# Sorted attention pairs: denominators stored as a 65th column of the row table, division after the read-back, numerators turned by VectorE, and plan points moved

## The chip, the cores and the metric

The kernel runs on one core of a Trainium2 chip. Five engines with in-order queues work side by side on that core: TensorE (PE in the profile, with its weight loads as PEld), VectorE (DVE), ScalarE (ACT), GpSimd (POOL) and SyncE (SP), which mostly issues DMAs. The metric is the device time of one execution in microseconds, lower being better. The kernel before takes 925.34 us as the median of three runs (924.95 to 927.41).

## The reference

The first stage is clustered attention, the second a hard-swish feed-forward network (FFN):

```
q, k, v: (4, 8, 768, 64) float32     centroids: (8, 16, 64)
q_assign = argmax_c(normalise(q) . normalise(centroids))      # per head, 16 clusters
k_assign = argmax_c(normalise(k) . normalise(centroids))
scores   = q k^T / 8, and -1e9 where q_assign != k_assign
attn     = softmax(scores);  attn_out = attn v
x   = attn_out as (4*768, 512)
h   = x w_in;  out = (h * clip(h + 3, 0, 6) / 6) w_out        # 512 -> 2048 -> 512
```

A query therefore attends only to the keys of its own cluster. Numerators (exp(scores) v) and denominators (the sum of exp(scores)) are formed apart, and their quotient goes to the FFN.

## The kernel before

The 32 heads are taken two at a time: 16 *pairs*, numbered 0 to 15 (`g`). Four pairs make one batch, and a batch can enter the FFN when its four pairs are done.

**Pairs 0 to 6** are done with the full 768 x 768 score matrix and a mask, in a first loop. This takes the first quarter of the run, together with decoding of the weights. **Pairs 7 to 15** (`FIRST` = 7, `SECOND` = 8) are *sorted*: the rows of q, k and v are written to DRAM tables in the order of their clusters, so that only a band around the diagonal has to be computed. A sorted pair passes these steps:

- `load_natural`, `turn_natural`, `cluster_scores`, `own_clusters`, `run_up`, `step_up`, `order`, `positions`: every token's cluster, and from it its row in sorted order (`pos`). `load_queries` and `load_keys` fetch the rows that are to be scattered.
- `scatter`: 24 indirect DMAs issued by POOL write the rows of q (`qd`) and of k and v (`kvd`) to DRAM in sorted order. Behind each stand three small memsets (`pause`). The first sorted pair's scatter runs in the first loop.
- `load_ranked` reads the sorted rows back: q and k as 32 x 32 blocks (`piece`), v as rows (`vs`). `turn_ranked` turns the blocks by VectorE's 32 x 32 block transpose into `xs`, features on partitions.
- `band_scores`, `band_values`, `key_adds`, `band_sums`: the band's exponentials, the numerators `bn` (features on partitions, tokens along the row), and the denominators `dn` (a row per head and half).
- `band_divide` (L1318): three PE transposes of `dn` (L1322) and six of `bn` (L1326) bring tokens onto partitions, VectorE takes the reciprocal (L1330) and multiplies in two halves (L1333) into `xr`.
- `keep_ranked` (L1340): two DMAs on SP's queue write `xr` to the DRAM tables `xsd`, 768 rows of 64 floats for each head.
- `gather` (L1193): 12 indirect DMAs issued by POOL read the rows of `xsd` in the original order into `xn`, each with a pause behind it.
- `turn_back` (L1345): six PE transposes through the PSUM tile `ps`, a copy by ACT (L1039) into `xt`, and a DMA to `xd`, from which the FFN loads its blocks (`load_block`, L577). Where the pair closes a batch, the batch's FFN items are appended to `fill`.

The PSUM pool of `ps`, `psum_s`, has one buffer in this stage. `band_scores`, `band_divide` and `turn_back` all use it. The SBUF pool `rowp` holds `bn`, `xr`, `xn` and `xt` under one tag in three buffers.

**What sets the order.** The order is written out by hand. `steps_of(g)` gives each step an offset; `late_plan` adds the pair's base (`AHEAD` = 38 plus `SLOT` = 29 for each pair behind pair 8; 6 for pair 7; two less for the last pair) and yields a list of *points*. The loop at L1573 goes through the points, issues the steps of a point, and then one FFN item from `fill`, except at two points of each slot (`busy`). An FFN item is half of an `up` (uX or uY, L709, with sums on VectorE, L720) or half of a `down` part (X or Y, L748). A block of 256 tokens has 8 `up` and 7 `down` parts, so 30 items. While `gating` holds, a point's steps are put off to the next. Behind the last point (263), what is left of `fill` runs: a rest of batch 2, then all of batch 3. `down`'s last part stores an output half on ACT's queue when `st["last"]` is set, else on SP's. ACT's queue also issues the loads of the kept weight sums `tx` (L595).

In the first loop, two score tiles make one step `n`, and twelve tiles a pair. At step 6 of a pair the next loads are issued (`load`, L1544), and `load_sums` inverts the denominators of batch 0 and lets its first FFN block be loaded, by way of functions put off from step to step (L523).

Of the kernel before, what the change touches and what calls it, by code (L numbers as in the profile page):

```python
# [17 lines left out]
C = 16  # L18
# [107 lines left out]
def fast_path(ctx, tc, ok, q, k, v, centroids, moe_w_in, moe_w_out, out):  # L126
# [380 lines left out]
    def load_sums(b):  # L507
        size = 2 * NCH
        tok = plain[:, NKT * b * size : (NKT * b + unsorted(b)) * size]
        nc.sync.dma_start(tok, st["sums", b].rearrange("k t s -> (k t s)").rearrange("(p n) -> p n", p=P))  # L510

        def invert():
            nc.vector.reciprocal(out=tok, in_=tok)
            nc.sync.dma_start(st["rd", b].rearrange("k t s -> (k t s)").rearrange("(p n) -> p n", p=P), tok)
            return complete

        def complete():
            if unsorted(b) == NKT:
                waiting.extend((b, m) for m in range(NHC))
                load_block()  # L520

        if b == 0:
            later.append(lambda: later.append(lambda wait=invert(): later.append(wait)))  # L523
        else:
            st["invert"], st["complete"] = invert, complete

# [108 lines left out]
    def ffn_items(b):  # L635
# [121 lines left out]
        def down(m, part):  # L757
# [33 lines left out]
            def end():  # L791
# [150 lines left out]
    def open_late():  # L942
# [249 lines left out]

    def gather(g):  # L1193
        pos = st["pos", g]
        xn = st["xn", g] = st["rowp"].tile([P, NCH, 2, D], F32, name="xn", tag="row")
        for t in range(2):
            for j in range(NCH):
                nc.gpsimd.indirect_dma_start(  # L1198
                    out=xn[:, j, t], out_offset=None, in_=rows["xsd", g, t],
                    in_offset=bass.IndirectOffsetOnAxis(ap=pos[:, 0, j, t : t + 1], axis=0),  # L1200
                )
                pause()
# [112 lines left out]
        for i in range(NCH):  # L1315
            st.pop(("be", g, i))

    def band_divide(g):  # L1318
        dn, bn = st.pop(("dn", g)), st.pop(("bn", g))
        pt = scratch([P, NHC, P], "pdt")  # L1320
        for i in range(NHC):
            nc.tensor.transpose(out=pt[:, i], in_=dn[:, i * P : (i + 1) * P], identity=ident)  # L1322
        ps = st["psum_s"].tile([P, 2, 512], F32, name="ps")
        for i in range(NCH):
            at = i % NHC * P
            nc.tensor.transpose(  # L1326
                out=ps[:, i // NHC, at : at + P], in_=bn[:, i // NHC, at : at + P], identity=ident
            )
        inv = inverses[:, g - FIRST]
        nc.vector.reciprocal(out=inv, in_=pt[:, :, 0 : P : 2 * C])  # L1330
        xr = st["rowp"].tile([P, NCH, 2, D], F32, name="xr", tag="row")
        for hf in range(2):
            nc.vector.tensor_tensor(  # L1333
                out=xr[:, hf * NHC : (hf + 1) * NHC],
                in0=ps[:, hf, 0:HALF].rearrange("p (i t d) -> p i t d", i=NHC, t=2),
                in1=inv[:, :, hf : 4 : 2].unsqueeze(3).to_broadcast([P, NHC, 2, D]), op=ALU.mult,
            )
        st["xr", g] = xr

    def keep_ranked(g):  # L1340
        xr = st.pop(("xr", g))
        for t in range(2):
            nc.sync.dma_start(ranked("xsd", g, t), xr[:, :, t])

    def turn_back(g):  # L1345
        xn = st.pop(("xn", g))
        st.pop(("pos", g))
# [13 lines left out]
    def steps_of(g):  # L1361

        first, last = g == SECOND, g == NPAIR - 1
        if first:
            plan = [
                (-38, load_queries), (-38, load_keys, 0), (-38, load_keys, 1),
            ]
        elif g == FIRST:
            plan = [(-6, lambda g: st.pop("signed")())]
        else:  # L1370
            plan = [
                (-52, load_natural, 1), (-51, load_natural, 0), (-46, turn_natural, 1), (-45, turn_natural, 0),
                (-42, cluster_scores), (-40, own_clusters), (-39, load_queries), (-39, run_up), (-38, step_up),
                (-36, load_keys, 0), (-35, order), (-34, positions), (-33, load_keys, 1),
            ]
        s = -37 if first else -30
# [10 lines left out]
        if last:  # L1387
            plan += [
                (1, band_scores, (0, 5), 1), (2, band_scores, (2,), 3), (3, band_scores, (4,)),
                (3, band_values, 0), (3, key_adds, 0, 1, 2), (4, key_adds, 0, 3), (5, band_values, 1),  # L1390
                (5, key_adds, 1, 1, 2), (6, key_adds, 1, 3), (8, band_sums), (9, band_divide), (10, keep_ranked),
                (11, gather), (24, turn_back),
            ]
# [103 lines left out]
    with tc.manual_schedule():  # L1497
# [24 lines left out]
        for n in range(0, total + lag_d + 2, 2):  # L1522
# [19 lines left out]
                prep.pop(0)()  # L1542
            if r == 6:
                load(g + 2, "q", "k")  # L1544
                load(g + 1, "v")
            if len(prep) > 1:
                prep.pop(0)()
# [410 lines left out]
```

## Time and profile before

| | |
|---|---|
| time of the profiled execution | 924.17 us |
| its span | 922.4 us |
| median of three runs | 925.34 us |
| PE busy | 895.6 us (97%) |
| DVE busy | 586.4 us (64%) |
| POOL busy | 600.1 us (65%) |
| ACT busy | 305.0 us (33%) |

The span runs from the first to the last instruction of the program, and the execution's time has 1.8 us around it. A group's row gives an engine, an operation, the tiles written and read, the count, then the busy time in us, the mean of one in ns, and the idle time of the engine just before it with what ended that. A row of the timeline gives a start, a length, and in brackets the idle time before it. A row of the windows gives, for each engine, its busy time in that stretch.

### The profile page before, as it was taken

Reading aid. Unit: us, or ns where it says so; the run is one execution under the profiler, and the core shown is the slowest. Engines: PE = TensorE matmul, PEld = TensorE weight load, DVE = VectorE, ACT = ScalarE, POOL = GpSimd, SP = SyncE. Lnnn points to the kernel's source line nnn. Section 1 sums busy time; section 2 is a strip of 40 time slices with the busy share of each in tenths; the row PEclk is TensorE's granted clock in tenths of the full one; section 3 lists DMA queues with packets and bytes.
Section 4 is the critical chain, followed back from the end, with each engine's and each line's share of the span. In section 5 each row is a group of like instructions: output and inputs, shape, how many; then the busy total and the mean of one; then the engine's idle time right before and its main releaser. Section 6 shows DMA issues by size and latency. Waiting matters only on the chain.

```text
span 922.4 us, 17421 instructions
## 1 busy us (share of the span) xinstructions
PE 895.6 (97%) x6131; PEld 701.4 (76%) x6131; DVE 586.4 (64%) x1373; ACT 305.0 (33%) x627; POOL 600.1 (65%) x1438
## 2 busy tenths in 40 slices
PE   8999999999999999999999999999999988999997
PEld 5444444657798797887977978978888878999996
DVE  5874898799787394693774855856744716445361
ACT  6888786651220322212222230321412201112120
POOL 3878899996867858787888777787886051203030
PEclk9999999999999999999999999999999999999999
DMA  6656666536769577593792954937635413233220
GB/s 178 169 154 170 174 186 186 160 98 136 199 165 197 134 182 152 151 238 89 185 216 79 223 110 140 236 102 172 160 108 132 122 42 111 88 83 102 63 64 28
DMA packets 248377, 131.06 MB, mean 142 GB/s; under 512 B 206972, under 2 KB 225816, under 8 KB 248280
## 3 DMA queue, kind: packets, MB, share of 16 engines
q1 hardware_dynamic: 224168, 81.22, 36.9%
q10 hardware_dynamic: 13744, 34.44, 13.5%
q0 software_dynamic: 10368, 14.18, 5.1%
q8 instruction: 51, 0.84, 0.4%
q14 instruction: 46, 0.38, 0.1%
HBM read 99.82 MB, written 29.97 MB: 141 GB/s over the span
## 4 chain that ended last, share of the span: by engine, by line
PE 48%; DVE 9%; DMA 4%; POOL 2%; issue 1%; ACT 1%; ACTq 0%; SPq 0%; DVEq 0%; POOLq 0%
PE Y L748 14%; PE uY L709 9%; PE X L748 9%; PE uX L709 8%; PE pv L1285 3%; PE ps L1228 2%; DMA tx<-td 2%; DVE g_sb L720 1%; DVE sx L720 1%; DVE g_sb L699 1%; DVE g_sb L541 1%; POOL xn L1198 1%; PE pv L1228 1%; PE pd L1309 1%; PE ps L1038 1%
## 5 line engine op out<-in xcount | busy, mean ns | idle before, releaser
L1198 POOL DMA_INDIRECT xn<-xsd,pos x108 | 106.7, 988 | 58.9 <-DMA xsd<-xr 29.3
L538 ACT ACTIVATE sx<-g_sb,half_c 128x512 f32<-128x512 f32 x88 | 63.6, 722 | 198.5 <-DVE g_sb L720 198.3
L1147 POOL MEMSET unread<- 128x1 f32 x972 | 102.3, 105 | 37.6
L699 POOL TENSOR_TENSOR g_sb<-g_sb 128x256 f32<-128x256 f32 x52 | 39.6, 783 | 118.7 <-DVE g_sb L541 117.6
L457 POOL TENSOR_TENSOR acc<-acc,ex 128x768 f32<-128x768 f32 x56 | 104.5, 1867 | 16.7 <-ACT ex L446 14.1
L1155 POOL DMA_INDIRECT qd<-qn,pos x96 | 98.1, 1022 | 20.0 <-issue 14.4
L1155 POOL DMA_INDIRECT kvd<-kvn,pos x96 | 95.5, 995 | 21.8 <-issue 21.8
L748 PE MATMUL X<-w_out_sb,g_sb 128*128 128x256 f32 x384 | 93.3, 387 | 1.5 <-DVE g_sb L541 1.4
L709 PE MATMUL uX<-xb,w_in_sb 128*128 128x128 f32 x704 | 93.0, 275 | 0.0
L748 PE MATMUL Y<-T,g_sb 128*128 128x256 f32 x384 | 88.5, 381 | 0.0
L748 PE MATMUL Y<-w_out_sb,g_sb 128*128 128x256 f32 x384 | 88.5, 381 | 0.0
L709 PEld LDWEIGHTS uX<-xb,w_in_sb 128*128 128x128 f32 x704 | 85.7, 192 | 0.0
L748 PEld LDWEIGHTS X<-w_out_sb,g_sb 128*128 128x128 f32 x384 | 71.7, 193 | 16.3 <-DVE g_sb L541 3.9
L748 PEld LDWEIGHTS Y<-w_out_sb,g_sb 128*128 128x128 f32 x384 | 72.2, 190 | 12.6 <-issue 2.7
L748 PEld LDWEIGHTS Y<-T,g_sb 128*128 128x128 f32 x384 | 72.0, 190 | 12.5 <-issue 2.7
L755 DVE TENSOR_TENSOR y<-y,Y 128x256 f32<-128x256 f32 x47 | 19.7, 420 | 92.7 <-PE Y L748 91.9
L720 DVE TENSOR_TENSOR sx<-uX,sx 128x128 f32<-128x128 f32 x176 | 50.7, 288 | 38.3 <-ACT sx L727 34.1
L423 PE MATMUL ps<-xf 64*128 64x384 f32 x336 | 68.8, 487 | 0.6 <-ACT ex L446 0.6
L720 DVE TENSOR_TENSOR g_sb<-uY,sx 128x128 f32<-128x128 f32 (+1 forms) x176 | 65.5, 413 | 0.2 <-DVE sx L720 0.2
L446 ACT ACTIVATE ex<-ps 128x768 f32<-128x768 f32 x84 | 63.7, 803 | 3.1 <-PE ps L423 2.6
L541 DVE SCALAR_TENSOR_TENSOR g_sb<-sx,g_sb 128x512 f32<-128x512 f32 x88 | 63.3, 722 | 2.0 <-ACT sx L538 2.0
L467 PE MATMUL pv<-ex,vt 128*64 128x384 f32 x336 | 63.5, 499 | 0.0
(228 smaller groups left out, 1723.7 us busy)
## 6 DMA issues: line engine op xcount, KB each, us to landing
tx<-td ACTq DMA_DIRECT2D x86, 384.0 KB
raw<-in_moe_w_in_dram SPq DMA_DIRECT2D x16, 512.0 KB
raw<-in_moe_w_out_dram SPq DMA_DIRECT2D x16, 512.0 KB
xb<-xd SPq DMA_DIRECT2D x12, 512.0 KB
out_dram<-y SPq DMA_DIRECT2D x44, 128.0 KB
piece<-qd SPq DMA_DIRECT2D x36, 96.0 KB
piece<-kvd SPq DMA_DIRECT2D x36, 96.0 KB
vs<-kvd SPq DMA_DIRECT2D x18, 192.0 KB
```

Source lines behind the costliest of these rows:

```text
L423: nc.tensor.matmul(st["ps", n][:, t, 0:HALF], lhsT=x[r, NCH + j], rhs=x[r, hf * NHC : (hf + 1) * NHC], start=first, stop=last, skip_group_ ...
L446: nc.scalar.activation(out=ex, in_=sc, func=ACT.Exp, scale=SM_SCALE)
L457: nc.gpsimd.tensor_tensor(out=acc, in0=acc, in1=ex, op=ALU.add)
L467: nc.tensor.matmul(pv[t * D : (t + 1) * D], lhsT=vt[:, t, j], rhs=ex[:, t], start=(j == 0), stop=(j == NCH - 1),)
L538: nc.scalar.activation(out=r, in_=h, func=ACT.Relu, bias=half_c, scale=1.0 / 6.0)
L541: nc.vector.scalar_tensor_tensor(out=g, in0=r, scalar=1.0, in1=h, op0=ALU.min, op1=ALU.mult)
L709: nc.tensor.matmul(dst, lhsT=w[:, kt], rhs=x(kt), start=(kt == 0), stop=(kt == HK - 1))
L720: nc.vector.tensor_tensor(out=out_, in0=in0, in1=in1, op=ALU.add)
L748: nc.tensor.matmul(bank[:, half * HC : (half + 1) * HC], lhsT=g_sb[:, kind, i], rhs=w[:, i], start=(first and i == 0), stop=(last and i == ...
L1147: nc.gpsimd.memset(unread, 0.0)
L1155: i = nc.gpsimd.indirect_dma_start(out=rows[name, g, t], in_=src[:, j, t].rearrange("p a d -> p (a d)") if a else src[:, j, t], in_offset= ...
L1198: nc.gpsimd.indirect_dma_start(out=xn[:, j, t], out_offset=None, in_=rows["xsd", g, t], in_offset=bass.IndirectOffsetOnAxis(ap=pos[:, 0, j ...
```

## The change

1. `band_divide` goes. `band_turn` turns the numerators in 32 x 32 blocks by one VectorE transpose. The denominators stay as they are.
2. `keep_ranked` writes undivided numerators, for each head two DMAs of 128-byte runs, and one DMA that writes the 768 sums as column 64 of the row table. Rows of `xsd` have 65 floats now.
3. `gather` reads rows of 65 floats. `weigh` (new, one call a head) takes the reciprocal of the gathered column and multiplies, from SBUF to SBUF, into `xw`, which `turn_back` turns.
4. `rowp` has four buffers.
5. Points: `band_turn` and `band_sums` at offset 11 (12 and 14 before), `keep_ranked` at 13 (16), pair 7's `gather` at 15 (17), `weigh` at 32 and 33, `turn_back` at 35 (37). Pair 8's steps behind its scatter come three points sooner. For pairs 9 and up the natural loads, turns and rank steps come one point sooner, but not `load_queries`, `load_keys`, `order` and `positions`. The last pair's steps from offset -20 on have a base that is five less (two before), its earlier steps none (two less before).
6. The last output half of a block goes by ACT's queue only for the last batch; in the first loop the values' load moves from step 6 to step 8, and batch 0's first block is released one step later.

```diff
-            ("wholep", 1), ("rowp", 3), ("posp", 3),
+            ("wholep", 1), ("rowp", 4), ("posp", 3),
...
-        for g in range(FIRST, NPAIR) for t in range(2) for name, w in (("qd", D), ("kvd", 2 * D), ("xsd", D))
+        for g in range(FIRST, NPAIR) for t in range(2) for name, w in (("qd", D), ("kvd", 2 * D), ("xsd", D + 1))
...
-    def band_divide(g):
-        dn, bn = st.pop(("dn", g)), st.pop(("bn", g))
-        pt = scratch([P, NHC, P], "pdt")
-        for i in range(NHC):
-            nc.tensor.transpose(out=pt[:, i], in_=dn[:, i * P : (i + 1) * P], identity=ident)
-        ps = st["psum_s"].tile([P, 2, 512], F32, name="ps")
...
-        nc.vector.reciprocal(out=inv, in_=pt[:, :, 0 : P : 2 * C])
...
+    def band_turn(g):
+        bn = st.pop(("bn", g))
+        xr = st["xr", g] = st["rowp"].tile([P, NCH, P], F32, name="xr", tag="row")
+        turn_blocks(bn.rearrange("p h c -> p (h c)"), xr)
+
+    def keep_ranked(g):
+        xr, dn = st.pop(("xr", g)).rearrange("p j c -> p (j c)"), st.pop(("dn", g))
+        for t in range(2):
+            dst = rows["xsd", g, t]
+            for x in range(2):
+                at = (2 * t + x) * Q
+                nc.sync.dma_start(
+                    dst.rearrange("(b r) d -> r b d", r=Q)[:, :, x * Q : (x + 1) * Q],
+                    xr[at : at + Q].rearrange("r (b i) -> r b i", i=Q),
+                )
+            nc.sync.dma_start(
+                dst[:, D : D + 1].rearrange("(h c) o -> h (c o)", h=2), dn[t * D : (t + 1) * D : 2 * C]
             )
...
+    def weigh(g, t):
+        xn = st["xn", g]
+        if t == 0:
+            st["xw", g] = st["rowp"].tile([P, NCH, 2, D], F32, name="xw", tag="row")
+        inv = inverses[:, g - FIRST].rearrange("p i c -> p (i c)")[:, t * NCH : (t + 1) * NCH]
+        nc.vector.reciprocal(out=inv, in_=xn[:, :, t, D])
+        nc.vector.tensor_tensor(
+            out=st["xw", g][:, :, t], in0=xn[:, :, t, 0:D],
+            in1=inv.unsqueeze(2).to_broadcast([P, NCH, D]), op=ALU.mult,
+        )
...
-                (9, key_adds, 1, 1, 2), (10, key_adds, 1, 3), (12, band_sums), (14, band_divide), (16, keep_ranked),
-                (17 if g == FIRST else 23, gather), (37, turn_back),
+                (9, key_adds, 1, 1, 2), (10, key_adds, 1, 3), (11, band_turn), (11, band_sums), (13, keep_ranked),
+                (15 if g == FIRST else 23, gather), (32, weigh, 0), (33, weigh, 1), (35, turn_back),
...
-                i = (AHEAD + SLOT * (g - SECOND) - 2 * (g == NPAIR - 1) if g > FIRST else 6) + offset
+                i = offset + {FIRST: 6, SECOND: 35}.get(g, AHEAD + SLOT * (g - SECOND))
+                if g == NPAIR - 1 and offset > -20:
+                    i -= 5
...
-                        keep(0, 1, y0[:, HC:], nc.scalar if st["last"] else nc.sync)
+                        keep(0, 1, y0[:, HC:], nc.scalar if b == B - 1 else nc.sync)
```

More of the change, by code (lines that the diff above doesn't have):

```diff
@@ L522, in load_sums @@
         if b == 0:
-            later.append(lambda: later.append(lambda wait=invert(): later.append(wait)))
+            later.append(lambda: later.append(lambda wait=invert(): later.append(lambda: later.append(wait))))
         else:
@@ L1194, in gather @@
         pos = st["pos", g]
-        xn = st["xn", g] = st["rowp"].tile([P, NCH, 2, D], F32, name="xn", tag="row")
+        xn = st["xn", g] = st["rowp"].tile([P, NCH, 2, D + 1], F32, name="xn", tag="row")
         for t in range(2):
@@ L1316, in band_sums @@
             st.pop(("be", g, i))
-    def band_divide(g):
-        dn, bn = st.pop(("dn", g)), st.pop(("bn", g))
-        pt = scratch([P, NHC, P], "pdt")
-        for i in range(NHC):
-            nc.tensor.transpose(out=pt[:, i], in_=dn[:, i * P : (i + 1) * P], identity=ident)
-        ps = st["psum_s"].tile([P, 2, 512], F32, name="ps")
[L1324 to L1327, printed above, removed]
-            )
[L1329 to L1343, printed above, removed]
+    def band_turn(g):
[14 more added lines that the diff above has]
+                dst[:, D : D + 1].rearrange("(h c) o -> h (c o)", h=2), dn[t * D : (t + 1) * D : 2 * C]
+            )
@@ L1345, in turn_back @@
+    def weigh(g, t):
[8 more added lines that the diff above has]
+        )
     def turn_back(g):
-        xn = st.pop(("xn", g))
@@ L1347, in turn_back @@
-        st.pop(("pos", g))
+        st.pop(("xn", g)), st.pop(("pos", g))
+        xn = st.pop(("xw", g))
         b, kt = divmod(g, NKT)
@@ L1365, in steps_of @@
             plan = [
-                (-38, load_queries), (-38, load_keys, 0), (-38, load_keys, 1),
+                (-35, load_queries), (-35, load_keys, 0), (-35, load_keys, 1),
             ]
@@ L1371, in steps_of @@
             plan = [
-                (-52, load_natural, 1), (-51, load_natural, 0), (-46, turn_natural, 1), (-45, turn_natural, 0),
-                (-42, cluster_scores), (-40, own_clusters), (-39, load_queries), (-39, run_up), (-38, step_up),
+                (-53, load_natural, 1), (-52, load_natural, 0), (-47, turn_natural, 1), (-46, turn_natural, 0),
+                (-43, cluster_scores), (-41, own_clusters), (-40, run_up), (-39, load_queries), (-39, step_up),
                 (-36, load_keys, 0), (-35, order), (-34, positions), (-33, load_keys, 1),
             ]
-        s = -37 if first else -30
+        s = -34 if first else -30
         if g == FIRST:
@@ L1390, in steps_of @@
                 (3, band_values, 0), (3, key_adds, 0, 1, 2), (4, key_adds, 0, 3), (5, band_values, 1),
-                (5, key_adds, 1, 1, 2), (6, key_adds, 1, 3), (8, band_sums), (9, band_divide), (10, keep_ranked),
-                (11, gather), (24, turn_back),
+                (5, key_adds, 1, 1, 2), (6, key_adds, 1, 3), (7, band_turn), (8, band_sums), (9, keep_ranked),
+                (10, gather), (19, weigh, 0), (25, weigh, 1), (27, turn_back),
             ]
@@ L1544, in fast_path @@
                 load(g + 2, "q", "k")
+            if r == 8:
                 load(g + 1, "v")
```

## The prediction

> **What bounds the kernel now.** I read the page's parts 1 and 2, then the windows by stage, the groups by line, and last the timelines of PE, POOL and SP around the steps that move.
>
> ```profile
> span 922.4 us, 17421 instructions
> ...
> PE   8999999999999999999999999999999988999997
> ```
>
> ```profile
> 610.00:668.00 58.00, 57.81 (x423) 49.26 (x421) 35.96 (x98) 13.96 (x30) 46.56 (x141) 1.00 0.58 143
> ```
>
> The first fence is PE's busy share in 40 slices, the second a window, with PE, PEld, DVE, ACT and POOL in that order. PE is full nearly everywhere and its order is fixed, so a us taken from PE's own work is a us of the end, unless something else comes late. In a stretch of one sorted pair (610 to 668) PE is busy for 57.8 of 58 us at a granted clock of 1.00, and DVE for 36, which leaves it 22. POOL shows 46.6, but its issue gaps are not in that:
>
> ```profile
> 335.01 0.98 POOL L1198 DMA_INDIRECT xn<-xsd,pos  x1 [7.03 <-ACT sx L727]
> ...
> 354.85 1.01 POOL L1155 DMA_INDIRECT qd<-qn,pos  x1 [0.66 <-issue]
> ...
> 651.89 1.20 POOL L1155 DMA_INDIRECT qd<-qn,pos  x1 [0.66 <-DVE g_sb L699]
> ...
> 690.07 0.97 POOL L1155 DMA_INDIRECT kvd<-kvn,pos  x1 [0.16 <-issue]
> ```
>
> From 354.85 (scatter of pair 10) to 651.89 (scatter of pair 15), five pairs, POOL goes from scatter to gather and on without a wait: 297.0/5 = 59.4 us a pair, about PE's own pace. So PE bounds the end and POOL stands right behind it: a shorter PE may meet POOL. PE's idle time is small outside the last gather.
>
> **The change, part by part.** *PE loses the nine transposes of nine pairs.*
>
> ```profile
> 725.31 0.55 PE L1322 MATMUL pdt<-ident,dn 128*128 128x128 f32 x3 [0.60 <-ACT dn L1314]
> 725.69 0.82 PE L1326 MATMUL ps<-ident,bn 128*128 128x128 f32 x6
> 726.34 0.61 PE L709 MATMUL uY<-xs,tx 128*128 128x128 f32 x4
> ```
>
> The lengths (0.55 + 0.82 = 1.37) hold pipelined ends that overlap the next work. From start to start the nine take 726.34 - 725.31 = 1.0 us, so 9 x 1.0 = 9.0 us go, and with them this wait for `dn`, 0.6. Bounds: 9.0 to 12.3 (9 x 1.37); I take 9.0, which is how PE's next work moves. Nothing covers for PE, so all of it counts.
>
> *PE gains a wait.* At offset 35 `turn_back` of one pair now stands directly ahead of the next pair's third `band_scores`, with no FFN item between, for pairs 7 and 9 to 13, by the changed program's PE order. Both want the one `ps` buffer. Before shows such a pair of neighbours once:
>
> ```profile
> 539.64 0.58 PE L1228 MATMUL ps<-xsort 64*128 64x240 f32 x4
> 540.27 0.97 ACT L1250 ACTIVATE be<-ps 128x960 f32<-128x960 f32 x1 [0.79 <-PE ps L1228]
> 541.29 0.33 PE L1228 MATMUL ps<-xmsort 64*128 64x352 bf16 x2 [0.33 <-ACT be L1250]
> 755.62 0.80 ACT L1039 COPY xt<-ps 128x768 f32<-128x768 f32 x1 [13.10 <-PE ps L1038]
> ```
>
> There `ps` was written until 540.22, ACT began 0.05 later, and PE went on 0.05 behind ACT's end; PE's other work hid most of that. Here nothing does: 0.80 for ACT's copy, 0.10 for the hand-overs, and 0.17 that the next work overlaps now (six transposes at 725.69: 0.82 - 0.65), 1.07 us, six times: 6.4 us. Bounds: 0 if ACT and PE find cover, 11 if ACT has an exponential of some 0.8 us ahead of the copy each time. Behind PE in that wait stands all PE work, so it counts fully.
>
> *The last gather and the last store queue.*
>
> ```profile
> L1038 PE MATMUL ps<-ident,xn 128*128 128x128 f32 x54 | 8.2, 279 | 3.4 <-DMA xn<-xsd,pos 3.4
> ```
>
> ```profile
> 730.24 1.25 SPq L1343 DMA_DIRECT2D xsd<-xr  x2
> 736.00 0.94 POOL L1198 DMA_INDIRECT xn<-xsd,pos  x1 [25.26 <-DMA xsd<-xr]
> 770.78 0.35 ACTq L761 DMA_DIRECT2D out_dram<-y  x1
> 774.59 0.68 PE L709 MATMUL uX<-xs,tx 128*128 128x128 f32 x4 [1.73 <-DMA tx<-td]
> ```
>
> Pair 15's gather starts at 736.00, 5.8 us behind the first `xsd` issue, and its rows reach PE late by 3.4 us. Its write now stands at point 245 and `turn_back` stays at 263: 18 points in place of 14, some 8 us more at about 59 us for a pair's 29 points. So the 3.4 us go. At 770.78 ACT's queue holds an output store that waited for DVE, and the load of `tx` behind it makes PE wait 1.73 us. That store (of batch 2) goes to SP's queue now, and the wait goes; SP has no load for PE close behind it. Bounds for the two: 0 to 5.1, I take 5.1.
>
> *DVE.* Away: a reciprocal and two multiplies; new: one block transpose, two reciprocals, two multiplies.
>
> ```profile
> L1016 DVE STREAM_TRANSPOSE xsort<-piece 128x768 f32<-128x768 f32 x18 | 17.4, 970 | 11.9 <-DMA piece<-qd 6.1 <-DMA piece<-kvd 5.8
> L1333 DVE TENSOR_TENSOR xr<-ps,inverses 128x384 f32<-128x384 f32 x18 | 9.2, 552 | 1.9 <-PE ps L1326 1.3
> L1330 DVE RECIPROCAL inverses<-pdt 128x12 f32<-128x12 f32 x9 | 2.0, 226 | 8.6 <-PE pdt L1322 8.6
> ```
>
> 0.23 + 2 x 0.55 = 1.33 becomes 0.97 + 2 x 0.23 + 2 x 0.55 = 2.53, or 1.2 us a pair and 10.8 in all. DVE's free 22 us a pair hide it, at a cost of 0; without that cover, 10.8. `weigh` can also wait, with the FFN's sums queued behind it, if a gather has not landed by offset 33. The closest is pair 14:
>
> ```profile
> 709.37 0.94 POOL L1198 DMA_INDIRECT xn<-xsd,pos  x1
> 728.13 0.82 PE L1038 MATMUL ps<-ident,xn 128*128 128x128 f32 x6
> ```
>
> Its gather ends at 710.3 and its `turn_back` runs at 728.1. The second `weigh` stands four points sooner (8 us), and eight pairs' transposes less are 8 us: 712, some 2 us to spare even if POOL and PE's new waits didn't help, which they do (below).
>
> *SP and the row table.* `keep_ranked` issues six DMAs, not two: at 1.25/2 us, 2.5 us more a pair on SP, hidden while nothing urgent is behind it. The four block stores have 768 runs of 128 bytes, the form in which `piece` is loaded. The column is new: 768 writes of 4 bytes from two partitions.
>
> ```profile
> q1 hardware_dynamic: 224168, 81.22, 36.9%
> q0 software_dynamic: 10368, 14.18, 5.1%
> 501.46 0.48 ACT L1314 COPY dn<-pd 128x384 f32<-128x384 f32 x1 [2.17 <-PE pd L1309]
> 513.56 0.97 POOL L1198 DMA_INDIRECT xn<-xsd,pos  x1 [0.71 <-issue]
> ```
>
> A packet of q1 takes 0.369 x 16 x 922.4/224168 = 24 ns at 362 bytes, one of q0 73 ns at 1368. A line through both gives 7 ns at 4 bytes. With two partitions working one after another each, 384 packets take 2.7 us by 7 ns or 9.3 us by 24 ns; over 16 engines, 0.3 to 1.2. The time to spare: pair 11's `dn` at 501.9 moves to about 499 (one item sooner, five pairs' transposes less, three waits more), and its gather to 509.6 (below): 10 us for 1 us of issue, the column, and some 4 us to landing (the 5.8 above less the 1.25 of issue). By 7 ns it is hidden; by 24 ns POOL is late by some 4 us. I take hidden, as 4 bytes are far below the mean packet.
>
> [...] No run of before has such a store.
>
> *POOL.* The same 12 gathers (0.94 us for 256-byte rows, 0.97 for 512-byte ones, so 260 bytes change nothing).
>
> ```profile
> 350.57 0.18 DVE L1138 TENSOR_SCALAR pos<-posf 128x24 int32<-128x24 f32 x1
> 689.40 2.16 SPq L1013 DMA_DIRECT2D piece<-qd  x4
> 692.36 3.91 SPq L1013 DMA_DIRECT2D piece<-kvd  x4
> 699.20 0.97 DVE L1016 STREAM_TRANSPOSE xsort<-piece 128x768 f32<-128x768 f32 x1
> 699.54 0.61 PE L709 MATMUL uY<-xs,tx 128*128 128x128 f32 x4
> 704.55 0.28 PE L1228 MATMUL ps<-xmsort 64*128 64x240 bf16 x2
> ```
>
> Pair 8's gather no longer waits 7.03, as its `xsd` is written some six points sooner. Pair 10's scatter is then held by its positions: 350.75 - 2.0 (two pairs' transposes) + 1.07 + 1.1 (from there to POOL's start) = 350.9 instead of 354.85, so POOL's train runs 4.0 us sooner. Pair 15's scatter, unmoved by the points, ends at 691.0 - 4.0 = 687.0. From that end to `xs` took 700.2 - 691.0 = 9.2 in before, or 7.4 if the four loads issue in 2.16 like those of `qd` and not in 3.91: 694.4 to 696.2. PE comes to pair 15's `band_scores`, now three items sooner, at 699.5 - 8.0 + 6.4 = 697.9. It just doesn't wait. That is the closest call: had PE no new wait, it would stand 3 to 5 us for POOL here, and most of that gain would be lost.
>
> *First loop.* Values and the first block load one step of two score tiles later.
>
> ```profile
> 131.97 0.53 SPq L577 DMA_DIRECT2D xb<-xd  x1
> 145.49 1.22 DVE L531 TENSOR_TENSOR xb<-xb,rb 128x1024 f32<-128x1024 f32 x1
> ```
>
> The block has 13.5 us from its issue to its first use, more than a step, which hides it; else DVE waits for it and PE may for DVE, by a few us. The values have until the next pair, several steps. The fourth `rowp` buffer matches the added tile `xw`. Cost 0 for all three.
>
> *Sum.* 922.4 - 9.0 - 0.6 - 5.1 + 6.4 = 914.1 us of span, 915.9 with the 1.8 around it. The profiled 924.17 stands 1.2 below the median of 925.34, so 917.0 in terms of medians.
>
> **The rivals.**
>
> *PE's new wait is covered.* Then the gains alone would give 910.6, but POOL holds pair 15 until 694.4 to 696.2 instead of 691.5, so 913.5 to 915.3. For it: PE hid most of the wait at 541.29. Against: there it had independent matmuls of the same step, and here none stand between.
>
> *New small waits of POOL, SP or DVE*, such as a column at 24 ns and a first read later by 4 us, or DVE's extra work met in places without slack: 918 to 923. For it: POOL has no free time in five pairs, and DVE's 10.8 us is not all in free places.
>
> *The column store decides, slower than before.* Each us by which the rows land later than the 10 us to spare holds the gather, and POOL, without free time, hands it on to pair 15 and to the end. 928 needs 11 us of slip and 2 of slack, a column of 5 + 13 = 18 us, or 47 ns a write, twice q1's mean packet. At three times it (28 us) the end is near 938, and `weigh` holds DVE too. For it: tiny writes, one by one from two partitions. Against: q1's 24 ns is the mean at 362 bytes, and less is moved here.
>
> [...]
>
> *The change doesn't act*: excluded for the transposes, which are gone from the program; it would end at 925.
>
> **How the numbers follow.** Forecast 0.50 (911 to 921 by its bounds), covered wait 0.13, small new waits 0.19, column slower 0.14, gains and losses that cancel near 925 0.04. The predicted time is 917.0. The range 909.5 to 925 leaves out the column case and little of the rest. No change means within 0.3% of 925.34, about what a measurement of this kernel can tell (922.6 to 928.1): faster 0.78 (forecast, covered wait and 0.15 of the small waits), same 0.08, slower 0.14.
>
> **What would show it.** L1322 and L1326 are absent, and PE's work is some 9 us less. The matmuls of `band_scores` behind `turn_back` show about 0.9 us of idle time each, ended by ACT's `xt`. Pair 8's gather follows its scatter at once; gathers of the last pair end ahead of `weigh`; no PE wait for `tx` near 770. It is wrong if POOL shows idle time ended by `xsd<-dn`, if DVE waits in `weigh`, or if PE waits over 3 us at pair 15's `band_scores`.

## The result, and the profile after

The changed kernel takes 993.6 us (median of 6 runs, 992.29 to 997.91) where the kernel before takes 925.14 (6 runs, 922.02 to 927.41). The ratio is 1.0747 with a 95% interval of 1.0721 to 1.0773: slower by 68 us, where 917.0 was forecast. The span of the profiled execution is 996.1 us.

The first fence is from the page of the kernel after: span and busy times, PE's busy share and the clock in 40 slices, q1's packets, and the chain that ended last.

```profile
span 996.1 us, 17342 instructions
...
PE 902.9 (91%) x6050; PEld 708.0 (71%) x6050; DVE 597.8 (60%) x1391; ACT 304.8 (31%) x627; POOL 597.1 (60%) x1438
...
PE   8999989999989889699599699698899997999997
...
PEclk9999998999989989899799799899899999999999
...
q1 hardware_dynamic: 252284, 81.41, 36.4%
...
PE 70%; DMA 13%; SPq 5%; DVE 5%; ACT 3%; issue 2%; POOL 2%; DVEq 0%; ACTq 0%; POOLq 0%
```

PE's row, nearly all nines before, falls to 5 or 6 tenths in slices 17, 20, 23 and 26, and the clock's row, all nines before, has a dent in these and in slices 7, 12, 15 and 29. PE's time outside its work (span less busy) went from 922.4 - 895.6 = 26.8 us to 93.2. The table of waits (engine, line, what it waited for: us in all, times, the longest) says for what:

```profile
ACT cs L365 <- DMA xsd<-dn: 95.2, 7, 18.2
...
PE pr L1057 <- ACT cs L365: 54.3, 7, 10.7
POOL xn L1198 <- DMA xsd<-dn: 38.4, 5, 9.0
...
DVE inverses L1342 <- DMA xn<-xsd,pos: 11.6, 2, 8.7
...
PE uX L709 <- DMA tx<-td: 8.7, 7, 1.7
...
PE ps L1228 <- ACT xt L1039: 5.3, 6, 0.9
...
PE ph L656 <- DVE xb L531: 4.7, 1, 4.7
...
PE ps L1038 <- DVE xw L1343: 2.7, 1, 2.7
PE ps L1228 <- DVE xsort L1016: 2.1, 1, 2.1
```

In the kernel before, ACT waits at L365 for PE alone:

```profile
ACT cs L365 <- PE pcs L356: 20.8, 12, 5.0
```

The first two lines of the table are one chain. ACT's copy of `cs` (the cluster scores of a later pair, L365) waits seven times for the store of the column of sums, `xsd<-dn`, and PE waits seven times for `cs`. Nothing in the computation connects the two. The buffers do:

```
L363   cs = st.get("rankp", rtp).tile([P, NC2 // 4, P], F32, name="cs", tag="third")
L1313  dn = st["dn", g] = st["rankp"].tile([P, HALF], F32, name="dn", tag="third")
```

`rankp` has one buffer for each tag, so `cs` and `dn` are the same memory. Before, PE's three transposes read `dn` within 3.1 us of its being written (pair 9: 382.61 to 385.71) and set it free. Now it is held until its column has landed in DRAM, and `cluster_scores` of the pair after next stands two points behind `keep_ranked` (five and nine points for pairs 7 and 8). One such place, where pair 9 stores, is shown by the timelines of SP, ACT and PE in turn (start, us, engine, line, tiles, and in brackets the idle time before and what ended it):

```profile
403.10 0.90 SPq L1329 DMA_DIRECT2D xsd<-xr  x2
404.09 0.60 SPq L1333 DMA_DIRECT2D xsd<-dn  x1
404.74 7.48 SPq L1329 DMA_DIRECT2D xsd<-xr  x2
412.26 1.54 SPq L1333 DMA_DIRECT2D xsd<-dn  x1
414.12 4.63 SPq L1020 DMA_DIRECT2D qn<-in_q_dram  x1
```

```profile
402.05 0.48 ACT L1314 COPY dn<-pd 128x384 f32<-128x384 f32 x1 [2.31 <-PE pd L1309]
...
421.56 0.48 ACT L365 COPY cs<-pcs 128x384 f32<-128x384 f32 x1 [14.27 <-DMA xsd<-dn]
```

```profile
411.93 0.61 PE L709 MATMUL uY<-xs,w_in_sb 128*128 128x128 f32 x4
422.09 0.90 PE L1057 MATMUL pr<-ident,cs 128*128 128x128 f32 x3 [9.56 <-ACT cs L365]
422.79 1.06 PE L709 MATMUL uX<-xs,tx 128*128 128x128 f32 x4
423.64 0.63 PE L709 MATMUL uX<-xb,w_in_sb 128*128 128x128 f32 x2
```

`dn` is written at 402.5. SP issues the second head's stores for 7.5 us in place of 0.9, since the first column stands in the queue (without it the same four stores take 3.2 us, see no_column). The second column is issued by 413.80 and lands by 421.56. Until then ACT, which works in order, does nothing, and PE is out of work from 412.54 to 422.09. The windows of the same stretch (PE, PEld, DVE, ACT, POOL busy; granted clock; DMA share; GB/s) show what follows:

```profile
414.00:415.70 1.70, 0.00 (x0) 0.00 (x0) 0.00 (x0) 0.00 (x0) 0.00 (x0) 1.00 0.22 6
415.80:420.00 4.20, 0.00 (x0) 0.00 (x0) 0.00 (x0) 0.00 (x0) 2.55 (x8) 0.50 0.28 24
...
426.00:430.00 4.00, 4.00 (x37) 4.00 (x37) 3.76 (x15) 0.00 (x0) 2.86 (x10) 0.99 0.65 146
```

```profile
422.20:426.00 3.80, 3.80 (x19) 3.80 (x20) 3.08 (x11) 1.60 (x4) 3.22 (x10) 0.50 1.07 232
```

In this place the clock fell to half 3.3 us after PE's last matmul (412.54 to 415.8) and came back 3.9 us after PE resumed (422.09 to 426.0), so the first 3.8 us of work ran at half pace: four matmuls at L709 take 1.06 us at 422.79 and 0.61 at 411.93. In the kernel before, half clock came after shorter waits: three of 1.07 to 1.19 us for the last gather between 751.07 and 755.11, with one transpose between each and the next, and then 0.50 in the window 755.00 to 758.40 (shown with points_in_before).

The sum of the difference, 73.7 us of span: 54.3 are the waits at L1057. Another 16.2 are put down to PE's work at half clock behind these waits and behind that at L656: PE is busy for 902.9 us here and for 886.7 in no_sums below, which has the same 6050 matmuls and not these waits. 8.9 are saved (895.6 before less 886.7); the kernel before and no_sums have short stretches of half clock of their own, so the last two numbers are good to some 2 us. The remaining 12.1 are the balance of the smaller waits that came and went (66.4 - 54.3).

### The profile page after: what moved, and what is told of

It is laid out like the page before. It is cut to its first block, busy times and chain, and to the rows that moved or that the text cites. A ratio compares the mean times of both kernels' runs of the same rounds, so it can differ in the third digit from the quotient of the medians.

```text
span 996.1 us, 17342 instructions
## 1 busy us (share of the span) xinstructions
PE 902.9 (91%) x6050; PEld 708.0 (71%) x6050; DVE 597.8 (60%) x1391; ACT 304.8 (31%) x627; POOL 597.1 (60%) x1438
## 3 DMA queue, kind: packets, MB, share of 16 engines
q1 hardware_dynamic: 252284, 81.41, 36.4%
q10 hardware_dynamic: 13600, 34.31, 12.4%
## 4 chain that ended last, share of the span: by engine, by line
PE 70%; DMA 13%; SPq 5%; DVE 5%; ACT 3%; issue 2%; POOL 2%; DVEq 0%; ACTq 0%; POOLq 0%
PE Y L748 14%; PE uY L709 12%; PE X L748 11%; PE uX L709 9%; DMA xsd<-dn 7%; PE ps L423 6%; PE pv L467 5%; SPq L1329 5%; DMA tx<-td 3%; PE pv L1285 3%; PE ph L656 3%; PE ps L1228 3%; PE pv L1228 1%; POOL xn L1198 1%; PE pqk L337 1%
## 5 line engine op out<-in xcount | busy, mean ns | idle before, releaser
L1198 POOL DMA_INDIRECT xn<-xsd,pos x108 | 104.3, 965 | 104.3 <-DMA xsd<-dn 38.4
L699 POOL TENSOR_TENSOR g_sb<-g_sb 128x256 f32<-128x256 f32 x52 | 38.4, 759 | 120.2 <-DVE g_sb L541 119.2
L709 PE MATMUL uX<-xb,w_in_sb 128*128 128x128 f32 x704 | 95.6, 280 | 0.0
L748 PE MATMUL Y<-w_out_sb,g_sb 128*128 128x256 f32 x384 | 91.2, 390 | 0.0
L748 PE MATMUL X<-w_out_sb,g_sb 128*128 128x256 f32 x384 | 90.5, 382 | 0.0
L709 PEld LDWEIGHTS uX<-xb,w_in_sb 128*128 128x128 f32 x704 | 88.2, 197 | 0.0
L748 PEld LDWEIGHTS Y<-w_out_sb,g_sb 128*128 128x128 f32 x384 | 73.8, 195 | 14.3 <-issue 3.8
L709 PE MATMUL uX<-xs,tx 128*128 128x128 f32 x352 | 57.0, 286 | 9.5 <-DMA tx<-td 8.7
```

Source lines behind the costliest of these rows:

```text
L709: nc.tensor.matmul(dst, lhsT=w[:, kt], rhs=x(kt), start=(kt == 0), stop=(kt == HK - 1))
L748: nc.tensor.matmul(bank[:, half * HC : (half + 1) * HC], lhsT=g_sb[:, kind, i], rhs=w[:, i], start=(first and i == 0), stop=(last and i == ...
L1198: nc.gpsimd.indirect_dma_start(out=xn[:, j, t], out_offset=None, in_=rows["xsd", g, t], in_offset=bass.IndirectOffsetOnAxis(ap=pos[:, 0, j ...
```

## The experiments

Each kernel was timed against the kernel before on its own chip, and its ratio is to that; it is estimated from the single runs and differs a little from the quotient of the medians. The theory was: the buffer that `dn` shares with `cs` is the main cause (A). The rival: the columns jam SP's queue and delay loads and gathers, and the buffer doesn't matter (B).

**The column alone, in the kernel before (column_in_before).**

```
+        dn = st.pop(("dn", g))                       # at the end of keep_ranked, behind the stores of xr
+        for t in range(2):
+            nc.sync.dma_start(
+                columns[g, t][:, D : D + 1].rearrange("(h c) o -> h (c o)", h=2), dn[t * D : (t + 1) * D : 2 * C]
+            )
```

> The kernel before, with one thing added: behind the two stores of a sorted pair's divided rows, the same two stores of dn's column into tables that nothing reads, and dn stays in the buffer that it shares with cs. The result is not changed. Theory A (the shared buffer): dn is held until both columns have landed, some 16 us behind its copy, and ACT's copy of cs for the pair after next, in the same step as the stores, waits for that. PE then idles in own_clusters (L1054 to L1060) by 7 to 14 us in each of the seven pairs 9 to 15, with a lowered clock behind each wait: 985 to 1005 us. Theory B (the columns only fill SP's queue, and the buffer doesn't matter): no wait of ACT at cs, and at most the 19 us by which own_buffer stands above no_column: 930 to 945 us.

Measured: 993.19 us, ratio 1.0701 (1.0633 to 1.0769), within A's range and far above B's. Its table of waits (L1058 is the L1057 of the kernel after):

```profile
ACT cs L365 <- DMA col<-dn: 88.8, 7, 20.0
...
PE pr L1058 <- ACT cs L365: 47.1, 6, 12.1
```

Two DMAs a pair of 768 numbers each, read by nobody, cost the kernel before about as much as the whole change (the two intervals overlap).

**A buffer of its own for dn (own_buffer)** (one of the four `rowp` buffers is given up for its space).

```
-            ("wholep", 1), ("rowp", 4), ("posp", 3),
+            ("wholep", 1), ("rowp", 3), ("posp", 3),
...
-        dn = st["dn", g] = st["rankp"].tile([P, HALF], F32, name="dn", tag="third")
+        dn = st["dn", g] = st["rankp"].tile([P, HALF], F32, name="dn", tag="sums")
```

> The changed kernel, but the denominators dn get a buffer of their own (one buffer, tag of its own) and no longer share one with the cluster scores cs and with prod; to make room, rowp has three buffers again. Theory A (the shared buffer): in the changed kernel ACT's copy of cs waits until the column store of dn has landed, PE waits 54.3 us for ACT at L1057 in seven pairs, and works some 15 us slower in the half-clock stretches behind those waits. Then these waits go here, and the time is 993.6 - 54 - 15 = 925, between 918 and 932. [...]

Measured: 939.23 us, ratio 1.0137 (1.0097 to 1.0177). 54 of the 68 us are gone, and with them every wait of `cs` for the column: ACT waits at L365 for PE alone. So A holds for the main part. It is not all: 939 is above the range, and the columns still stand in the queue. SP's timeline of own_buffer:

```profile
386.11 1.13 SPq L1329 DMA_DIRECT2D xsd<-xr  x2
387.32 0.56 SPq L1333 DMA_DIRECT2D xsd<-dn  x1
387.94 6.52 SPq L1329 DMA_DIRECT2D xsd<-xr  x2
394.50 0.58 SPq L1333 DMA_DIRECT2D xsd<-dn  x1
395.40 7.91 SPq L1020 DMA_DIRECT2D qn<-in_q_dram  x1
```

SP is held for 17.2 us (386.11 to 403.31) with six stores and the first load behind them.

**No column at all (no_column).** Rows of 64, no store of `dn`, and `weigh` takes reciprocals of ones. The kernel leaves out the division, so its output isn't the reference's; it has four `rowp` buffers like the changed kernel.

```
-            nc.sync.dma_start(
-                dst[:, D : D + 1].rearrange("(h c) o -> h (c o)", h=2), dn[t * D : (t + 1) * D : 2 * C]
-            )
...
-        nc.vector.reciprocal(out=inv, in_=xn[:, :, t, D])
+        nc.vector.reciprocal(out=inv, in_=ones[:, 0:NCH])
```

> The changed kernel without the column: rows of 64 floats, no store of the sums, and weigh takes the reciprocals of ones, so the sorted pairs' numerators go to the FFN undivided. Theory A: as nobody but ACT touches dn, its buffer is free at once; PE's waits at L1057 go, 915 to 930, within 5 us of the run with dn's own buffer. Theory B: SP's queue is free of the column, 915 to 925, and far below the run with dn's own buffer. What this run is below that one is the column's own cost in queues.

Measured: 920.17 us, ratio 0.9949 (0.9917 to 0.9982). The same place on SP's queue:

```profile
385.75 3.23 SPq L1329 DMA_DIRECT2D xsd<-xr  x4
389.29 0.66 SPq L1020 DMA_DIRECT2D qn<-in_q_dram  x1
```

The four block stores take 3.2 us and the load behind them 0.7. So B is real as well, and worth up to what stands between this kernel and own_buffer: 939.23 - 920.17 = 19 us. In own_buffer no single wait of PE holds them; PE's time outside its work is larger by 15.5 us (939.2 - 892.0, against 918.9 - 887.2), spread over small waits for `tx`, for VectorE and for the gathers, and its work by 4.8 us (892.0 - 887.2). Own_buffer also has one `rowp` buffer less than no_column; what that costs by itself was not tried.

**The column from 32 partitions (spread_column, spread_again).** VectorE turns `dn` by blocks into a buffer `dt` of its own, and each head's column goes out in two DMAs of 12 numbers from each of 32 partitions. In `keep_ranked` the name `dn` now stands for `dt`; `rowp` has three buffers, as in own_buffer.

```
+        dt = st["dt", g] = st["rankp"].tile([P, HALF], F32, name="dt", tag="sums")
+        nc.vector.transpose(out=dt, in_=dn)
...
-            nc.sync.dma_start(
-                dst[:, D : D + 1].rearrange("(h c) o -> h (c o)", h=2), dn[t * D : (t + 1) * D : 2 * C]
-            )
+            for x in range(2):
+                at = (2 * t + x) * Q
+                nc.sync.dma_start(
+                    dst.rearrange("(h b r) d -> h r b d", h=2, r=Q)[x][:, :, D : D + 1],
+                    dn[at : at + Q].rearrange("r (b i) -> r b i", i=Q)[:, :, 0:1],
+                )
```

> The changed kernel, but VectorE turns the sums in 32 x 32 blocks first (into a buffer of its own, rowp with three buffers), and the column is stored from 32 partitions by 12 writes each, in two DMAs a head. [...] Theory A: PE's waits at L1057 go, as with dn's own buffer: 918 to 930. Theory B: only the spread helps, the same range. [...]

> spread_column once more, on the chip of the two other kernels of this call. If the chips differ little: 1.005 of the kernel before, as in the first run. If spread_first_loop's 1.0165 came from a chip on which loads land later: 1.01 to 1.02 here too, where the kernel before takes 928 or more.

Measured: 930.33 us, ratio 1.0053 (1.0025 to 1.0081), and 928.07, ratio 1.0035 (1.0004 to 1.0065), on a second chip. SP's timeline of the second:

```profile
393.41 5.14 SPq L1337 DMA_DIRECT2D xsd<-dt  x2
398.87 0.66 SPq L1020 DMA_DIRECT2D qn<-in_q_dram  x1
```

The load behind the last column issues in 0.66 us again in place of 7.91. But the second head's two column stores themselves take 5.14 here, and SP is held for 12.4 us in all (387.17, the first block store, to 399.53), against 17.2 in own_buffer and 4.2 in no_column. The same number of 4-byte writes, from 32 partitions in place of two, took 9 us less than in own_buffer (939.23 - 930.33), but is still no gain on the kernel before. Why the load behind a column issues sooner was not shown: no view here counts the engines of one DMA. The queue's packets show the writes: q1 has 252284 - 238424 = 13860 more in the changed kernel than in no_column, and 252824 - 238424 = 14400 more in spread_column, where 18 columns have 18 x 768 = 13824 numbers. The spread didn't make the writes cheaper in all: by the pages q1's share is 0.420 x 927.2 = 389 us on the mean of the 16 engines here, for 0.391 x 939.2 = 367 in own_buffer and for 0.377 x 918.9 = 346 in no_column. Why is open.

**The first loop as before (first_loop_as_before).** Both edits of the first loop undone in the changed kernel.

```
-            later.append(lambda: later.append(lambda wait=invert(): later.append(lambda: later.append(wait))))
+            later.append(lambda: later.append(lambda wait=invert(): later.append(wait)))
...
-            if r == 8:
                 load(g + 1, "v")
```

> The changed kernel, with the two edits of the first loop undone (values loaded at step 6, batch 0's first block released one step sooner). If the 4.68 us of PE idle time at 146 us, ended by DVE's first multiply that waits for rb, comes from these edits, the time falls by 4.7 us and 1 to 3 us of half clock behind it: 986 to 988. If the block's load was late for another reason (SP's or DVE's order), it stays at 993.6.

Measured: 991.69 us, ratio 1.0702 (1.0665 to 1.0740). The wait of 4.7 us at L656 is gone (1.9 us of waiting for VectorE stand there), but the time is above the 986 to 988 expected and the intervals of the two kernels overlap, so its worth is not settled by this run.

**Spread column with the first loop as before (spread_first_loop), and without the neighbours on ps (spread_no_neighbour).** The second also moves `turn_back` from offset 35 to 37, so that FFN work stands ahead of the next pair's `band_scores`.

```
-                (15 if g == FIRST else 23, gather), (32, weigh, 0), (33, weigh, 1), (35, turn_back),
+                (15 if g == FIRST else 23, gather), (32, weigh, 0), (33, weigh, 1), (37, turn_back),
```

> spread_column with both edits of the first loop undone (values load and first block as in the kernel before). If the gap of 4.63 us at 145.9 is caused by them alone: it is gone, and 930.3 falls by 4 to 7 us (4.63 and the slower clock behind it): 923 to 927. If other waits take it up, as in first_loop_as_before, where only some 2 us were won: 927 to 930.

> As spread_first_loop, with turn_back at offset 37 in place of 35, so that FFN work stands between it and the next pair's band_scores, which write the same ps buffer. If the six waits of 0.89 us at L1228 are the cost of the neighbours: they are gone, and the time is 5.3 us below spread_first_loop, some 918 to 922. If PE only waits elsewhere instead (turn_back later makes FFN blocks later): no gain, 923 to 927.

Measured: 944.87 us, ratio 1.0165 (1.0087 to 1.0242), and 939.33, ratio 1.0080 (1.0034 to 1.0126). Both ran on a chip on which the kernel before took 929.75 (923.27 to 936.39) and all kernels scattered more, so their times don't compare with the 930 and 928 above. Of the six waits of 0.89 us for `xt`, the first shows five (4.4 us; a sixth of 0.9 us is put down to issue) and the second none; by time the intervals overlap. Inconclusive.

**No 4-byte writes (wide_rows, wide_again).** A table row has 66 columns, 32 numerators and a sum twice. VectorE writes the sums, times 1 or 0 by the half of the ranks, beside the numerators, and the four block stores carry them. The kernel also has the two edits of spread_no_neighbour (first loop as before, `turn_back` at 37) and three `rowp` buffers.

```
+        for h in range(2):
+            nc.vector.tensor_scalar(
+                out=st["xr", g][:, h * (S // Q // 2) : (h + 1) * (S // Q // 2), Q : Q + 1], in0=first,
+                scalar1=sides[:, h : h + 1], scalar2=None, op0=ALU.mult,
+            )
...
+                nc.sync.dma_start(
+                    dst.rearrange("(b r) d -> r b d", r=Q)[:, :, x * R : (x + 1) * R], xr[at : at + Q]
+                )
```

> As spread_no_neighbour, but no store of 4-byte items at all: a row of the table has 66 columns, 32 numerators and a sum twice, VectorE writes the sums (times 1 or 0, by the half that a rank is in) beside the numerators, and the four block stores of a pair carry them in runs of 132 bytes. weigh adds the two sums first. It costs DVE some 0.5 us more a pair. If the 4-byte writes are what is left of the column's cost (spread_column stands 10 us above no_column): 920 less 5.3 for the neighbours and 2 to 5 for the first loop: 910 to 914. If it is the number of stores, the division behind the gather or VectorE's work: no better than spread_no_neighbour, 918 to 922 or more.

> wide_rows once more beside spread_again and the floor below. If the 4-byte writes are the cost that is left: below spread_again by 5 to 15 us (the neighbour waits of 5.3 and what the column still costs). If the block stores of 128 bytes or so and the later loads of tx are: no better than spread_again.

**No sums (no_sums).** This is no_column with two edits shown above, the first loop as before and `turn_back` at 37. It leaves out the division as well, and has four `rowp` buffers.

> no_column with the first loop as in the kernel before and turn_back at offset 37: rows of 64 numerators, no sums stored, so the sorted pairs' rows are not divided by their sums (weigh multiplies by reciprocals of ones). It is the time that the change would have with sums that cost nothing. By the six waits of 0.89 us and the gap of 4.67 at 146 that no_column still had (920.2): 910 to 915, or 0.985 of the kernel before. If PE waits for tx in their place: 918 to 922.

Measured: wide_rows 940.69 us on the scattering chip, ratio 1.0102 (1.0066 to 1.0138); on the other, beside spread_again, 926.46, ratio 1.0022 (1.0004 to 1.0039), no better than spread_again by the intervals. no_sums on the same chip: 913.74, ratio 0.9884 (0.9860 to 0.9908). So the 4-byte writes are not the cost that is left: without them the sums still cost 926.46 - 913.74 = 12.7 us. The pages' rows of queue q1 (packets, MB, share of 16 engines' span), wide_again and then no_sums:

```profile
q1 hardware_dynamic: 238424, 81.46, 40.3%
```

```profile
q1 hardware_dynamic: 238424, 81.35, 37.9%
```

With as many packets the queue's engines are busy for 0.403 x 921.0 - 0.379 x 912.3 = 25 us more, on the mean of the 16. PE's waits for `tx` take 10.5 us in the first and 3.9 in the second:

```profile
PE uX L713 <- DMA tx<-td: 10.5, 7, 4.5
```

```profile
PE uX L709 <- DMA tx<-td: 3.9, 4, 1.6
```

Whether it is runs of 132 bytes in place of 128, rows of 264 in place of 256, the gathers of such rows, VectorE's 609.3 - 595.0 = 14.3 us more work, or the one `rowp` buffer less, was not tried and stays open.

**The last pair's points alone, in the kernel before (points_in_before).** Its points stand two sooner, `turn_back` stays, and batch 2's output store goes to SP's queue.

```
-                (11, gather), (24, turn_back),
+                (11, gather), (26, turn_back),
...
+                if g == NPAIR - 1 and offset > -20:
+                    i -= 2
...
-                        keep(0, 1, y0[:, HC:], nc.scalar if st["last"] else nc.sync)
+                        keep(0, 1, y0[:, HC:], nc.scalar if b == B - 1 else nc.sync)
```

> The kernel before, with the last pair alone moved: its points behind -20 stand two sooner, turn_back stays where it is, and batch 2's output store goes to SP's queue as in the changed kernel. It tests step (last gather and last store queue) by itself. If that step is right: the waits of 3.4 us at L1038 (last gather) and 1.73 us at 772.9 (tx) are gone, some 920 us or 0.994 of the kernel before. If pair 15's rows are not sorted in time for its earlier band_scores (xs was ready at 700.2 in the kernel before), PE waits there by up to 4 us: 924 to 926.

Measured: 919.37 us, ratio 0.9946 (0.9927 to 0.9965). It is the one kernel here that does the whole computation and is faster than the kernel before. Its page and waits:

```profile
span 915.3 us, 17423 instructions
...
PE 891.9 (97%) x6131; PEld 699.7 (76%) x6131; DVE 587.6 (64%) x1373; ACT 305.3 (33%) x627; POOL 598.6 (65%) x1438
```

```profile
PE uX L709 <- DMA tx<-td: 1.4, 4, 0.6
...
PE ps L1038 <- PE uY L709: 0.4, 1, 0.4
```

The wait for the last gather is gone, and the longest for `tx` is 0.6 in place of 1.73. PE's busy time fell by 3.7 us as well, with the same matmuls: before, the last gather's waits were followed by a stretch at a clock of 0.50 (the window 755.00 to 758.40 of the kernel before), which isn't there now. It accounts for some 1.6 of the 3.7 us (3.29 us of work at half pace); the rest is not explained.

```profile
755.00:758.40 3.40, 3.29 (x9) 2.67 (x10) 0.00 (x0) 0.80 (x1) 0.00 (x0) 0.50 0.29 116
```

## Why the prediction was wrong

The step that failed is "SP and the row table": the column "is hidden". It failed in two places.

*Who waits for the column.* The step counted the gather and POOL as its only waiters and gave them 10 us. The reader of `dn` changed from PE, which was done with it after 3.1 us, to two DMAs that hold it for 19 us (402.5 to 421.56), and the step didn't ask what is written next into `dn`'s buffer. The line that makes the tile says it (L1313, tag "third"), five lines above the code that was changed; the other user of the tag stands at L363. This mechanism stood in none of the rivals. It cost 54.3 us of idle time and, by the half clock behind it, some 14 more (an estimate: the 16.2 less the 2.6 behind L656, below); column_in_before and own_buffer show it from both sides. The sign named for this step, POOL idle until `xsd<-dn`, did show (38.4 us), but the larger loss went by ACT and `cs`, for which no sign was named.

*How long the column takes.* The step took 7 ns a write and 2.7 us, with 24 ns and 9.3 us as the other end. Measured: the second column was issued at 413.80 and had landed by 421.56, 7.8 us, which is 20 ns a write by the step's own count (two partitions side by side, 384 writes each). That count was the author's assumption, and no run shows that the two go side by side. The value taken was far too low, and for one column the upper end was near. But a pair has two columns, one for each head, and the step counted one. They go one behind the other: from 404.69, where the first is issued, to 421.56, where the second has landed, are 16.9 us. Two columns at 24 ns are 18.6 us, past the 18 us at which the rival "the column store decides" put 928; with the second column counted, the prediction's own upper price already reached that rival. A line through two points at 362 and 1368 bytes was no ground for a price at 4 bytes. Jamming SP's own issue behind it wasn't in the sum at all; with the gathers it is part of the 19 us between own_buffer and no_column. That rival had the right suspect, but with the gather (and `weigh` behind it) as its only way to the end and 47 ns a write, for one column, as its threshold.

The other steps, in their order:

- *Nine transposes of nine pairs, 9.0 us.* Right: PE's work falls from 895.6 to 886.7 us (no_sums), 8.9, with 81 matmuls fewer, and to the same 2 us as said above.
- *PE's new wait for ps, 1.07 x 6 = 6.4.* The mechanism and the six places were right; the size is 0.89 x 6 = 5.3 of idle time. The rival that it is covered falls, as the waits stand with `turn_back` at 35 and are gone with it at 37.
- *Last gather and last store queue, 5.1.* Right by itself: 924.72 - 919.37 = 5.35 in the kernel before, and both waits are gone. That the size fits so well is in part luck: in the profiles PE's idle time fell by 3.4 us only (26.8 to 915.3 - 891.9), as other waits grew, and PE's work by 3.7, which the step didn't count. In the changed kernel the gain was eaten: there `weigh` waits 8.7 us for the last gather, and PE 2.7 for `weigh`.
- *DVE, 10.8 us more and hidden.* Its busy time grew by 597.8 - 586.4 = 11.4. What of it shows in PE's waits can't be told apart from the column's delays in the changed kernel; in no_sums, where they are absent, no wait of PE for `weigh` is left.
- *POOL and pair 15, "just doesn't wait".* PE waits 2.1 us there (L1228 for `xsort`) in the changed kernel, where POOL itself lost 38.4 us to the column. In no_column, where PE has its new waits as the step assumed, it doesn't wait there, so the step held. In no_sums, without these waits, it waits 0.6 us, not the 3 to 5 that the step named for that case.
- *First loop at 0.* Mis-sized: 4.7 us of PE's idle time, and some 2.6 more behind it (5.2 us of work between 150.60 and 155.90 at a clock of 0.50). I had looked at the block `xb` alone; behind it stand two loads of `rb`, and these land last:

```profile
138.03 1.30 SPq L581 DMA_DIRECT2D rb<-rd  x2
148.04 2.51 DVE L531 TENSOR_TENSOR xb<-xb,rb 128x1024 f32<-128x1024 f32 x1 [4.66 <-DMA rb<-rd]
150.69 1.62 PE L656 MATMUL ph<-xb,w_in_sb 128*128 128x256 f32 x3 [4.68 <-DVE xb L531]
```

"By a few us" was the bound, and it should have been the value.

Without the column the sum holds, as far as that kernel stands for the rest of the change (it leaves out the column's stores and the division): 920.17 measured in no_column against 917.0, and the 4.7 us of the first loop are more than the difference.

## What to carry to other kernels

When a change gives a tile another reader, look up the tile's pool, tag and number of buffers, and ask who writes that buffer next and how long the new reader holds it: here the store's issue was over at 413.80, and the buffer's next writer began at 421.56, when the store had landed. Take the price of a store of single numbers from a run that has one, and look at what stands behind it on its queue: 768 of them from two partitions, 3 KB, took 7.8 us from issue to landing here, and the load behind them issued in 7.91 us in own_buffer, against 0.66 behind four block stores of 96 KB each, issued in 3.23 us, in no_column. And look at what follows a long wait of PE: behind the shortest of the seven here, 3.08 us, the clock was 0.50 from 283.50 to 287.40.

## What the runs showed of the hardware

That stores of 3 KB would slow the issue of what stands next on their queue was not expected: in the place shown of own_buffer two block stores took 6.52 us behind the first column and the load behind the second took 7.91, where no_column has 3.23 us for four block stores and 0.66 for the load. With the same numbers stored from 32 partitions the next load issued in 0.66 (spread_again), though the last column stores themselves took 5.14 to issue there. PE's long waits cost more than their length: in the place shown the clock was 0.50 from 3.3 us after the last matmul until 3.9 us after the next, and PE's work is 902.9 us in the changed kernel against 886.7 for the same matmuls in no_sums, on top of the waiting. Sums carried inside runs of 132 bytes, with as many packets as the 128-byte runs (238424), went with 25 us more of q1's time on the mean of its 16 engines (wide_again against no_sums); the reason is open.
